# Sliding-window attention and a feed-forward: batch t+1 of the attention issued between the products of feed-forward tile t

## The chip, the core and the metric

The kernel runs on one core of a Trainium2 chip. Its time is the device time of one execution in microseconds (us). The engines of the core are TensorE (PE: matrix products, their weight loads shown apart as PEld), VectorE (DVE), ScalarE (ACT), GpSimd (POOL) and SyncE (SP, which only issues transfers here). [...]

## What is computed

q, k and v are [8, 8, 576, 64] in float32 (batch, head, position, head dimension). Each position attends to the 32 before and the 32 behind it, the result goes through a feed-forward of 512 to 2048 to 512 with the tanh form of gelu:

```
scores = q @ k.transpose(0, 1, 3, 2) / sqrt(64)
scores = where(abs(i - j) <= 32, scores, -1e9)
attn   = softmax(scores, axis=-1)
x = (attn @ v).transpose(0, 2, 1, 3).reshape(4608, 512)
h = x @ w_in                                             # [4608, 2048]
g = 0.5 * h * (1 + tanh(sqrt(2 / pi) * (h + 0.044715 * h * h * h)))
out = g @ w_out                                          # [4608, 512], float32
```

## The kernel before

It has two stages, one after the other. The attention loops over 32 pairs of heads (`for hp in range(NP)`). For a pair, SP loads q and k and GpSimd loads v (lines 143 to 147, v turned into fp16 on the way) in chunks of 128 positions. VectorE casts q and k to fp16 (L170, L171), TensorE transposes them (L175) and VectorE copies them back from PSUM (L177). For each head, TensorE multiplies each of five 128-key chunks with the 192 queries around it (L191: 64 rows of the array, as the head dimension is 64), ACT takes the exponential (L198), GpSimd multiplies with the band mask `bm` (L199), and TensorE multiplies the result with `vst`, which holds 64 columns of v and 64 columns of ones (L204): so 64 output partitions hold the sum over v, and 64 the sum of the weights. VectorE copies the latter (L206), ACT forms its reciprocal as exp(-ln) (L209, L211), and VectorE writes the product to `xT` (L214), the transposed input of the feed-forward, [128, 4, 4608] in fp16.

The feed-forward loops over 9 tiles of 512 tokens (L223). For each of 16 blocks of 128 hidden units, four products with `w_in16` (L228) make `ph`; ACT squares it (L232), VectorE forms the argument of a sigmoid (L234), ACT takes the sigmoid (L236), VectorE multiplies with `ph` (L237) into `gT`. For each of four blocks of 128 tokens, 16 products with `w_out16` (L241) make `py`; VectorE copies it (L244) and SP stores it (L245).

PSUM is split by stage: the attention's pools are closed before the feed-forward's is opened. The order of instructions on each engine is made by a scheduler that may move them: it sets products of L241 of one block between those of L228 of the next. The exponential and the logarithm share a table set that is loaded at the start (L65); the feed-forward's functions need another one.

Of the kernel before, what the change touches and what calls it, by code (L numbers as in the profile page):

```python
# [9 lines left out]
FP32 = mybir.dt.float32  # L10
FP16 = mybir.dt.float16
BF16 = mybir.dt.bfloat16
AF = mybir.ActivationFunctionType
ALU = mybir.AluOpType

_A = 0.044715
_K1 = 1.5957691216057308
_K3 = _K1 * _A
_C = 1.0 / _A

WINDOW = 32


@with_exitstack
def kernel(
# [9 lines left out]
    nc = tc.nc  # L35
    B, H, S, D = q.shape
    DM, DF = moe_w_in.shape
    NTOK = B * S
    NP = B * H // 2
    SCALE = 1.0 / float(D) ** 0.5  # L40
    assert S == 576 and D == 64 and DM == 512 and DF == 2048

    KC = 128
    NKC = 5
    QW = KC + 2 * WINDOW
    nky = [128, 128, 128, 128, 64]
    qws = [0, 96, 224, 352, 480]
    qwn = [192, 192, 192, 192, 96]
    scol = [0, 192, 384, 576, 768]

    qf = q.rearrange("b h s d -> (b h s d)")
    kf = k.rearrange("b h s d -> (b h s d)")
    vf = v.rearrange("b h s d -> (b h s d)")
# [3 lines left out]
    sb = ctx.enter_context(tc.tile_pool(name="sb", bufs=3))  # L57
    sbq = ctx.enter_context(tc.tile_pool(name="sbq", bufs=3))
    att_ctx = ExitStack()
    psA = att_ctx.enter_context(tc.tile_pool(name="psA", bufs=2, space=bass.MemoryType.PSUM))  # L60
    psO = att_ctx.enter_context(tc.tile_pool(name="psO", bufs=2, space=bass.MemoryType.PSUM))

    _tabs = list(get_activation_tables(nc.m.arch).keys())
    _set_id = _tabs.index("natural_log_exp_and_others")
    nc.scalar.add_instruction(mybir.InstLoadActFuncSet(  # L65
        name=nc.get_next_instruction_name(), act_func_set_id=_set_id, ins=[], outs=[]))

    idn = const.tile([128, 128], FP32, name="idn")
# [3 lines left out]
    idn16 = const.tile([128, 128], FP16, name="idn16")  # L72
    nc.vector.tensor_copy(idn16, idn)
    bm = const.tile([128, NKC, QW], FP16, name="bm")
    nc.gpsimd.memset(bm, 1.0)
    nc.gpsimd.affine_select(out=bm[:, 0, :], in_=bm[:, 0, :], compare_op=ALU.is_ge,
                            fill=0.0, base=32, pattern=[[1, QW]], channel_multiplier=-1)
    nc.gpsimd.affine_select(out=bm[:, 0, :], in_=bm[:, 0, :], compare_op=ALU.is_ge,
                            fill=0.0, base=32, pattern=[[-1, QW]], channel_multiplier=1)
    for kc in range(1, NKC):  # L80
        nc.gpsimd.affine_select(out=bm[:, kc, :], in_=bm[:, kc, :], compare_op=ALU.is_ge,
                                fill=0.0, base=0, pattern=[[1, QW]], channel_multiplier=-1)
        nc.gpsimd.affine_select(out=bm[:, kc, :], in_=bm[:, kc, :], compare_op=ALU.is_ge,
                                fill=0.0, base=64, pattern=[[-1, QW]], channel_multiplier=1)
    nc.gpsimd.affine_select(out=bm[:, 4, :], in_=bm[:, 4, :], compare_op=ALU.is_ge,
                            fill=0.0, base=63, pattern=[[0, QW]], channel_multiplier=-1)
    nc.gpsimd.affine_select(out=bm[:, 4, :], in_=bm[:, 4, :], compare_op=ALU.is_ge,
                            fill=0.0, base=95, pattern=[[-1, QW]], channel_multiplier=0)

    w_in16 = big.tile([128, 4, DF], FP16, name="w_in16")  # L90
    w_out16 = big.tile([128, 16, DM], FP16, name="w_out16")
    nc.gpsimd.dma_start(w_in16, moe_w_in.rearrange("(c p) f -> p c f", p=128))
    nc.gpsimd.dma_start(w_out16, moe_w_out.rearrange("(c p) f -> p c f", p=128))

    xT = big.tile([128, 4, NTOK], FP16, name="xT")

    raw = []
    for kc in range(NKC):
        lo = max(0, kc * KC - WINDOW)
        hi = min(S, kc * KC + nky[kc] + WINDOW)  # L100
        if lo < 512 < hi:
            raw.append((kc, lo, 512))
            raw.append((kc, 512, hi))
        else:
            raw.append((kc, lo, hi))
    segsA, segsB = [], []
    fA = fB = None
    for (kc, lo, hi) in raw:
        if lo < 512:
            if fA is None:  # L110
                segsA.append((kc, lo, hi, True)); fA = hi
            else:
                if lo < fA:
                    segsA.append((kc, lo, min(hi, fA), False))
                if hi > fA:
                    segsA.append((kc, max(lo, fA), hi, False)); fA = hi
        else:
            if fB is None:
                segsB.append((kc, lo, hi, True)); fB = hi
            else:  # L120
                if lo < fB:
                    segsB.append((kc, lo, min(hi, fB), False))
                if hi > fB:
                    segsB.append((kc, max(lo, fB), hi, False)); fB = hi
    od_segs = [(kc, a, b_, st, False) for (kc, a, b_, st) in segsA[:-1]] \
        + [segsA[-1][:3] + (segsA[-1][3], True)] \
        + [(kc, a, b_, st, False) for (kc, a, b_, st) in segsB[:-1]] \
        + [segsB[-1][:3] + (segsB[-1][3], True)]

    for hp in range(NP):  # L130
        b = hp // 4
        pb = hp % 4
        hA = 2 * pb

        qst = sb.tile([128, NKC, 2, 64], FP32, name="qst")
        kst = sb.tile([128, NKC, 2, 64], FP32, name="kst")
        vst = sbq.tile([128, NKC, 2, 128], FP16, name="vst")
        nc.gpsimd.memset(vst[:, :, :, 64:128], 1.0)
        for h2 in range(2):
            hh = (b * H + hA + h2)  # L140
            base = hh * S * D
            if hh < B * H - 1:
                nc.sync.dma_start(qst[:, :, h2, :],  # L143
                                  qf[base:base + 640 * 64].rearrange("(c p d) -> p c d", p=128, d=64))
                nc.sync.dma_start(kst[:, :, h2, :],  # L145
                                  kf[base:base + 640 * 64].rearrange("(c p d) -> p c d", p=128, d=64))
                nc.gpsimd.dma_start(vst[:, :, h2, 0:64],  # L147
                                    vf[base:base + 640 * 64].rearrange("(c p d) -> p c d", p=128, d=64))
            else:
                nc.sync.dma_start(qst[:, 0:4, h2, :],  # L150
                                  qf[base:base + 512 * 64].rearrange("(c p d) -> p c d", p=128, d=64))
                nc.sync.dma_start(qst[0:64, 4, h2, :],
                                  qf[base + 512 * 64:base + 576 * 64].rearrange("(p d) -> p d", d=64))
                nc.sync.dma_start(kst[:, 0:4, h2, :],
                                  kf[base:base + 512 * 64].rearrange("(c p d) -> p c d", p=128, d=64))
                nc.sync.dma_start(kst[0:64, 4, h2, :],
                                  kf[base + 512 * 64:base + 576 * 64].rearrange("(p d) -> p d", d=64))
                nc.gpsimd.dma_start(vst[:, 0:4, h2, 0:64],
                                    vf[base:base + 512 * 64].rearrange("(c p d) -> p c d", p=128, d=64))
                nc.gpsimd.dma_start(vst[0:64, 4, h2, 0:64],  # L160
                                    vf[base + 512 * 64:base + 576 * 64].rearrange("(p d) -> p d", d=64))
                nc.vector.memset(vst[64:128, 4, h2, 0:64], 0.0)
                nc.vector.memset(qst[64:128, 4, h2, :], 0.0)
                nc.vector.memset(kst[64:128, 4, h2, :], 0.0)

        QT = sbq.tile([128, 704], FP16, name="QT")
        KT = sbq.tile([128, 704], FP16, name="KT")
        qst16 = sbq.tile([128, NKC, 2, 64], FP16, name="qst16")
        kst16 = sbq.tile([128, NKC, 2, 64], FP16, name="kst16")
        nc.vector.tensor_copy(qst16, qst)  # L170
        nc.vector.tensor_copy(kst16, kst)  # L171
        for (stg, dst) in ((qst16, QT), (kst16, KT)):
            ptr = psA.tile([128, 1024], FP16, name="ptr", tag="SP")
# [102 lines left out]
```

## Time and profile before

| | before |
|---|---|
| median of 3 runs | 559.22 us (557.71 to 559.3) |
| profiled execution, span | 556.9 us |
| PE busy | 414.3 us (74%), 2560 products |
| DVE busy | 413.5 us (74%) |
| ACT busy | 261.9 us (47%) |
| POOL busy | 211.0 us (38%) |
| bytes moved | 40.29 MB, mean 72 GB/s |

The span runs from the first to the last instruction of the profiled execution. A busy PE is counted to the modelled end of each product, so products that overlap are counted once. "L228" is line 228 of the kernel. Text behind "<-" in a row's brackets names the engine and the line whose work ended the idle time ahead of the row.

### The profile page before, as it was taken

To read this page: it belongs to the slowest core of one execution; us is meant where nothing else is said; L and a number is where in the kernel's file an instruction comes from. 1 tells how busy PE (TensorE), PEld (TensorE's weight loads), DVE (VectorE), ACT (ScalarE), POOL (GpSimd) and SP (SyncE) were. 2 spreads that over 40 slices of the span, in tenths; PEclk is the share of its full clock that TensorE was granted. 3 is DMA by queue.
4 is the path that set the end of the run, shared out by engine and by line. 5 is a ranking of instruction groups with operands and counts; after the bars stand their busy time and mean duration, and the time that the engine had idled before them with its cause. 6 is when DMAs were issued, how large, how long until landed. Compare 5 with 4: busy or idle time off the path is not lost.

```text
span 556.9 us, 7306 instructions
## 1 busy us (share of the span) xinstructions
PE 414.3 (74%) x2560; PEld 228.6 (41%) x2560; DVE 413.5 (74%) x648; ACT 261.9 (47%) x418; POOL 211.0 (38%) x182
## 2 busy tenths in 40 slices
PE   0134666666666776665569999999999999999996
PEld 0123455444444554444334444344444443434342
DVE  2027877788888888888658686878878787868685
ACT  0112443334344434344347474747566574747472
POOL 7415988788998888888700000000000000000000
PEclk9999999999999999999999999999999999999999
DMA  8999467677668776753100201010010202020202
GB/s 179 200 191 209 65 84 95 95 113 102 102 101 118 118 105 102 114 69 24 14 0 1 75 1 57 21 57 20 17 58 2 75 2 75 2 75 1 75 2 76
DMA packets 133621, 40.29 MB, mean 72 GB/s; under 512 B 126416, under 2 KB 128464, under 8 KB 133584
## 3 DMA queue, kind: packets, MB, share of 16 engines
q1 hardware_dynamic: 89056, 30.39, 22.4%
q0 software_dynamic: 44528, 9.43, 19.0%
q8 instruction: 20, 0.33, 0.2%
q14 instruction: 17, 0.14, 0.1%
HBM read 39.80 MB, written 9.44 MB: 88 GB/s over the span
## 4 chain that ended last, share of the span: by engine, by line
PE 63%; DVE 21%; SPq 5%; issue 4%; DMA 3%; ACT 3%; DVEq 0%; ACTq 0%
PE py L241 22%; PE ph L228 21%; PE ps_od L204 12%; DVE kst L171 9%; PE ps_s L191 5%; DVE Dbuf L206 4%; PE ptr L175 3%; SPq L143 3%; DMA qst<-in_q_dram 2%; SPq L145 2%; DVE xT L214 2%; DVE gT L237 1%; DVE qst L170 1%; DVE uu L234 1%; ACT sq L232 1%
## 5 line engine op out<-in xcount | busy, mean ns | idle before, releaser
L199 POOL TENSOR_TENSOR PT<-PTr,bm 128x960 f16<-128x960 f16 x64 | 129.7, 2042 | 66.5 <-PE ps_od L204 43.4
L228 PE MATMUL ph<-xT,w_in 128*128 128x512 f16 x576 | 143.5, 383 | 14.1 <-DVE gT L237 10.2
L241 PE MATMUL py<-w_out,gT 128*128 128x512 f16 x576 | 141.0, 379 | 0.4 <-DVE yo L244 0.3
L232 ACT ACTIVATE sq<-ph 128x512 f16<-128x512 f32 x144 | 84.9, 589 | 79.0 <-PE ph L228 78.9
L234 DVE SCALAR_TENSOR_TENSOR uu<-sq,ph 128x512 f16<-128x512 f16 x144 | 98.3, 684 | 24.9 <-ACT sq L232 24.9
L198 ACT ACTIVATE PTr<-ps_s 128x960 f16<-128x960 f32 x64 | 58.8, 967 | 102.8 <-PE ps_s L191 88.8
L237 DVE SCALAR_TENSOR_TENSOR gT<-sg,ph 128x512 f16<-128x512 f16 x144 | 98.4, 684 | 11.4 <-ACT sg L236 6.8
L236 ACT ACTIVATE sg<-uu 128x512 f16<-128x512 f16 x144 | 90.3, 627 | 26.2 <-DVE uu L234 26.2
L228 PEld LDWEIGHTS <-w_in 128*128 128x128 f16 x576 | 56.5, 98 | 87.9 <-issue 26.6
L204 PE MATMUL ps_od<-PT,vst 128*128 128x64 f16 (+5 forms) x704 | 75.9, 251 | 13.7 <-DVE xT L214 13.7
L241 PEld LDWEIGHTS <-gT 128*128 128x128 f16 x576 | 54.8, 98 | 71.8 <-DVE gT L237 8.9
L204 PEld LDWEIGHTS <-vst 128*128 128x128 f16 (+1 forms) x704 | 59.8, 125 | 36.4 <-issue 23.4
L191 PE MATMUL ps_s<-QT,KT 64*128 64x192 f16 (+2 forms) x384 | 41.5, 330 | 43.8 <-DVE KT L178 38.8
L206 DVE COPY Dbuf<-ps_od 64x576 f32<-64x576 f32 x64 | 48.6, 760 | 28.9 <-PE ps_od L204 28.8
L175 PE MATMUL ptr<-idn,kst 128*128 128x128 f16 x160 | 23.0, 309 | 56.2 <-DVE kst L171 48.3
L171 DVE CAST kst<-kst 128x640 f16<-128x640 f32 x32 | 54.9, 1715 | 12.3 <-DMA kst<-in_k_dram 11.6
L209 ACT ACTIVATE Lt<-Dbuf 128x576 f32<-128x576 f32 x32 | 21.9, 683 | 75.7 <-DVE Dbuf L206 74.2
L147 POOL DMA_DIRECT2D vst<-in_v_dram x63 | 55.9, 889 | 0.0
L214 DVE TENSOR_TENSOR xT<-ps_od,Rt 64x576 f16<-64x576 f32 x64 | 47.1, 736 | 5.2 <-ACT Rt L211 4.2
L191 PEld LDWEIGHTS <-KT 64*128 64x128 f16 x384 | 28.5, 130 | 52.9 <-DVE KT L178 45.9
L244 DVE COPY yo<-py 128x512 f32<-128x512 f32 x36 | 23.2, 686 | 26.9 <-PE py L241 26.9
L170 DVE CAST qst<-qst 128x640 f16<-128x640 f32 x32 | 26.6, 831 | 20.5 <-DMA qst<-in_q_dram 19.6
(32 smaller groups left out, 146.6 us busy)
## 6 DMA issues: line engine op xcount, KB each, us to landing
qst<-in_q_dram SPq DMA_DIRECT2D x63, 160.0 KB, 3.5
kst<-in_k_dram SPq DMA_DIRECT2D x63, 160.0 KB, 3.1
out_dram<-yo SPq DMA_DIRECT2D x36, 256.0 KB, 2.1
vst<-in_v_dram POOLq DMA_DIRECT2D x63, 80.0 KB, 3.8
w_in<-in_moe_w_in_dram POOLq DMA_DIRECT2D x1, 2048.0 KB, 15.4
w_out<-in_moe_w_out_dram POOLq DMA_DIRECT2D x1, 2048.0 KB, 27.4
qst<-in_q_dram SPq DMA_DIRECT2D x1, 128.0 KB, 3.5
kst<-in_k_dram SPq DMA_DIRECT2D x1, 128.0 KB, 3.2
```

The costliest lines, as they stand in the source:

```text
L171: nc.vector.tensor_copy(kst16, kst)
L191: nc.tensor.matmul(ps_f[:, c0 + a:c0 + b_], KT[r0:r0 + 64, kc * KC:kc * KC + KC], QT[r0:r0 + 64, qws[kc] + a:qws[kc] + b_], start=True, st ...
L198: nc.scalar.activation(PTr, ps_s5, AF.Exp, scale=SCALE)
L199: nc.gpsimd.tensor_tensor(PT, PTr, bm, op=ALU.mult)
L204: nc.tensor.matmul(ps_od[:, a:b_], vst[0:nky[kc], kc, pi, :], mv, start=st, stop=lastf)
L206: nc.vector.tensor_copy(Dbuf[r0:r0 + 64, :], ps_od[64:128, 0:S])
L228: nc.tensor.matmul(ph, w_in16[:, dc, fc * 128:fc * 128 + 128], xT[:, dc, tt * 512:(tt + 1) * 512], start=(dc == 0), stop=(dc == 3))
L232: nc.scalar.activation(sq, ph, AF.Square)
L234: nc.vector.scalar_tensor_tensor(uu, sq, _C, ph, ALU.add, ALU.mult)
L236: nc.scalar.activation(sg, uu, AF.Sigmoid, scale=_K3)
L237: nc.vector.scalar_tensor_tensor(gT[:, fc, :], sg, 1.0, ph, ALU.mult, ALU.mult)
L241: nc.tensor.matmul(py, gT[:, fc, tc4 * 128:tc4 * 128 + 128], w_out16[:, fc, :], start=(fc == 0), stop=(fc == 15))
```

## The change

The two stages become one program in a fixed order (the scheduler no longer moves instructions). The attention of batch 0 comes first. Then feed-forward tile t is written with the attention of batch t+1 inside it, for t from 0 to 6; tiles 7 and 8 have none. In the tile's first half, the 16 blocks of products with `w_in`, stand casts and transposes; in its second half, 16 steps of four products with `w_out`, stand `scores` and `values` of eight units (a pair of heads and one half of the queries each).

The queries are stored in a strided order (column j*144 + p holds position 4p + j), so that a load of q or k has runs of 1 KB, and the output rows are stored back by the same rule. A unit multiplies three key chunks with 40, 48 and 16 columns of four strides, for two heads on 64 rows of the array each. Values are multiplied with 64 columns of v or of ones for two heads, each with its own 64 columns of the array and its own half of PSUM's partitions. The mask product moves from GpSimd to VectorE; the reciprocal of the sums is read from PSUM by ACT without a copy. Gelu becomes one ACT instruction, so the table set changes twice in each tile with attention; one load is written out at the start of its second half.

PSUM is shared: three banks for `ph` and `py`, two for the scores (one buffer), two for the values (one buffer), one for transposes.

```
-    for hp in range(NP):                 # the attention loop of before, lines 130 to 215
-        ...
-            nc.scalar.activation(sq, ph, AF.Square)
-            nc.vector.scalar_tensor_tensor(uu, sq, _C, ph, ALU.add, ALU.mult)
-            nc.scalar.activation(sg, uu, AF.Sigmoid, scale=_K3)
-            nc.vector.scalar_tensor_tensor(gT[:, fc, :], sg, 1.0, ph, ALU.mult, ALU.mult)
...
+PIECES = {
+    0: [(0, 0, 40), (1, 24, 72), (2, 56, 72)],
+    1: [(2, 72, 104), (3, 88, 136), (4, 120, 144)],
+}
...
+    psM = ctx.enter_context(tc.tile_pool(name="psM", bufs=3, space=PSUM))
+    psS = ctx.enter_context(tc.tile_pool(name="psS", bufs=1, space=PSUM))
+    psO = ctx.enter_context(tc.tile_pool(name="psO", bufs=1, space=PSUM))
+    psT = ctx.enter_context(tc.tile_pool(name="psT", bufs=1, space=PSUM))
+    ctx.enter_context(tc.manual_schedule(engines=None))
...
+    load_qk(0, 4)
+    ...
+    load_v(0)
+    for i in range(4):
+        nc.gpsimd.dma_start(w_in16[:, :, 512 * i:512 * i + 512], w_in_v[:, :, 512 * i:512 * i + 512])
+    for h in range(2):
+        ...                               # two masks, memset on VectorE, 13 selects on GpSimd
+    for i in range(4):
+        nc.gpsimd.dma_start(w_out16[:, 4 * i:4 * i + 4, :], w_out_v[:, 4 * i:4 * i + 4, :])
+    ...
+    load_qk(1, 1)
+    load_v(1)
...
+    def cast_pair(b, pr):
+        qr, kr, tr = raws[b]
+        ...
+        for src, dst in ((qr, q16), (kr, k16)):
+            nc.vector.tensor_copy(
+                dst.rearrange("p j h d -> p h j d"),
+                src[:, 2 * pr:2 * pr + 2, :].rearrange("p h (j d) -> p h j d", j=4))
+
+    def trans_pair(b, pr):
+        q16, k16 = halfs.pop((b, pr))
+        pt = psT.tile([128, 8, 128], FP16, name="pt", tag="T")
+        for j in range(4):
+            nc.tensor.transpose(pt[:, j, :], q16[:, j, :, :], idn)
+        for j in range(4):
+            nc.tensor.transpose(pt[:, 4 + j, :], k16[:, j, :, :], idn)
+        nc.vector.tensor_copy(QTs[b][:, pr, :, 0:128], pt[:, 0:4, :])
+        nc.vector.tensor_copy(
+            KTs[b % 2][:, pr, 0:512].rearrange("d (p j) -> d p j", j=4),
+            pt[:, 4:8, :].rearrange("d j p -> d p j"))
+
+    def scores(b, u):
+        pr, hf = u // 2, u % 2
+        ps = psS.tile([128, 2, 512], FP32, name="ps_s")
+        off = 0
+        for (c, p0, p1) in PIECES[hf]:
+            n = p1 - p0
+            for h in range(2):
+                r0 = 64 * h
+                nc.tensor.matmul(
+                    ps[:, h, off:off + 4 * n].rearrange("k (j p) -> k j p", j=4),
+                    KTs[b % 2][r0:r0 + 64, pr, 128 * c:128 * c + 128],
+                    QTs[b][r0:r0 + 64, pr, :, p0:p1],
+                    start=True, stop=True)
+            off += 4 * n
+        pe = ap_.tile([128, 2, SW], FP16, name="pe")
+        nc.scalar.activation(pe, ps[:, :, 0:SW], AF.Exp, scale=SCALE)
+        pm = ap_.tile([128, 2, SW], FP16, name="pm")
+        nc.vector.tensor_tensor(
+            pm, pe, masks[hf].rearrange("p (o w) -> p o w", o=1).broadcast_to([128, 2, SW]),
+            op=ALU.mult)
+        units[(b, u)] = pm
+
+    def values(b, u):
+        ...
+        od = psO.tile([128, 2, 512], FP32, name="ps_od")
+        ...
+        for i, (c, p0, p1) in enumerate(PIECES[hf]):
+            ...
+            for w in range(2):
+                for h in range(2):
+                    r0 = 64 * h
+                    nc.tensor.matmul(
+                        od[r0:r0 + 64, w, 0:4 * HALF].rearrange("d (j p) -> d j p", j=4)[:, :, a:e],
+                        V[:, c, 2 * pr + h, :] if w == 0 else ones,
+                        pm[:, h, off:off + 4 * n].rearrange("k (j p) -> k j p", j=4),
+                        start=(i == 0), stop=(i == last), skip_group_check=True)
+            off += 4 * n
+        lt = ap_.tile([128, 4 * HALF], FP32, name="lt")
+        nc.scalar.activation(lt, od[:, 1, 0:4 * HALF], AF.Ln)
+        rt = ap_.tile([128, 4 * HALF], FP32, name="rt")
+        nc.scalar.activation(rt, lt, AF.Exp, scale=-1.0)
+        nc.vector.tensor_tensor(
+            xT[:, pr, b * S:(b + 1) * S].rearrange("d (j p) -> d j p", j=4)[:, :, HALF * hf:HALF * hf + HALF],
+            ...
+
+    def ffn_in(t, fc):
+        ...
+        ph = psM.tile([128, 512], FP32, name="ph", tag="mm")
+        for dc in range(4):
+            nc.tensor.matmul(ph, w_in16[:, dc, fc * 128:fc * 128 + 128],
+                             xT[:, dc, t * 512:(t + 1) * 512],
+                             start=(dc == 0), stop=(dc == 3))
+        nc.scalar.activation(gTs[t][:, fc, :], ph, AF.Gelu_apprx_tanh)
...
+    cast_tail(0)
+    for pr in range(NPAIR):
+        cast_pair(0, pr)
+        trans_pair(0, pr)
+        if pr == 0:
+            trans_tail(0)
+        for u in (2 * pr, 2 * pr + 1):
+            scores(0, u)
+            if u > 0:
+                values(0, u - 1)
+    values(0, 7)
+
+    for t in range(NT):
+        b = t + 1
+        att = b < B
+        if att and b + 1 < B:
+            load_qk(b + 1, 1)
+            load_v(b + 1) if b + 1 >= 2 else None
+        for fc in range(NF):
+            if att:
+                if fc == 1:
+                    cast_tail(b)
+                    cast_pair(b, 0)
+                if fc == 2:
+                    trans_tail(b)
+                if fc in (4, 7, 10, 13):
+                    pr = (fc - 4) // 3
+                    trans_pair(b, pr)
+                    if pr < 3:
+                        cast_pair(b, pr + 1)
+            ffn_in(t, fc)
+        sched = {}
+        if att:
+            load_exp_table()
+            for u in range(8):
+                sched.setdefault((3 * u) // 2, []).append((scores, u))
+                sched.setdefault((3 * u) // 2 + 2, []).append((values, u))
+        for i in range(16):
+            for fn, u in sched.get(i, []):
+                fn(b, u)
+            ffn_out(t, i // 4, 4 * (i % 4), 4 * (i % 4) + 4)
```

`cast_tail` and `trans_tail` do the same for the last 64 positions of all heads: one cast, four transposes and five copies. `load_qk` issues transfers of q and k on SP, `load_v` five of v on GpSimd. `ffn_out` makes four products of one 128-token block per call, and copies and stores the block at its fourth call.

## Rows read from the trace of the kernel before

**Rows 1.** Busy us (instructions) by stage, then granted clock, DMA share, GB/s.

```profile
46.00:285.68 239.68, 146.32 (x1316) 109.00 (x1315) 197.45 (x298) 97.69 (x123) 189.18 (x149) 1.00 0.65 90
285.68:553.80 268.12, 256.77 (x1152) 111.19 (x1152) 205.06 (x324) 158.28 (x289) 0.00 (x0) 1.00 0.09 35
```

**Rows 2.** Timeline of a pair of heads: start us, us, engine, line, tiles, count.

```profile
158.20 1.28 PE L191 MATMUL ps_s<-QT,KT 64*128 64x192 f16 x12 [0.59 <-DVE KT L178]
159.41 2.26 PEld L204 LDWEIGHTS <-vst 128*128 128x128 f16 x22 [0.30 <-issue]
159.41 2.36 PE L204 MATMUL ps_od<-PT,vst 128*128 128x160 f16 x22
161.02 3.96 POOL L199 TENSOR_TENSOR PT<-PTr,bm 128x960 f16<-128x960 f16 x2
161.70 0.71 PE L175 MATMUL ptr<-idn,qst 128*128 128x128 f16 x5
...
167.25 1.28 PE L191 MATMUL ps_s<-QT,KT 64*128 64x192 f16 x12 [0.59 <-DVE KT L178]
```

**Rows 3.** Chain of waits, the same piece of two tiles: start us, us, what.

```profile
410.50 1.73 PE ph L228 x8
...
439.94 1.73 PE ph L228 x8
```

**Rows 4.** Timeline at a tile's boundary and at the end of the kernel.

```profile
438.48 1.02 PE L228 MATMUL ph<-xT,w_in 128*128 128x512 f16 x4 [1.20 <-DVE gT L237]
...
549.46 3.61 PE L241 MATMUL py<-w_out,gT 128*128 128x512 f16 x16 [0.35 <-DVE yo L244]
...
553.11 0.69 DVE L244 COPY yo<-py 128x512 f32<-128x512 f32 x1 [2.51 <-PE py L241]
```

**Rows 5.** Groups by line: tiles, shapes, count, busy us, mean ns, idle before.

```profile
L234 DVE SCALAR_TENSOR_TENSOR uu<-sq,ph 128x512 f16<-128x512 f16 x144 | 98.3, 684 | 24.9 <-ACT sq L232 24.9
L236 ACT ACTIVATE sg<-uu 128x512 f16<-128x512 f16 x144 | 90.3, 627 | 26.2 <-DVE uu L234 26.2
L232 ACT ACTIVATE sq<-ph 128x512 f16<-128x512 f32 x144 | 84.9, 589 | 79.0 <-PE ph L228 78.9
L198 ACT ACTIVATE PTr<-ps_s 128x960 f16<-128x960 f32 x64 | 58.8, 967 | 102.8 <-PE ps_s L191 88.8 <-POOL vst L138 14.0
L147 POOL DMA_DIRECT2D vst<-in_v_dram x63 | 55.9, 889 | 0.0
L171 DVE CAST kst<-kst 128x640 f16<-128x640 f32 x32 | 54.9, 1715 | 12.3 <-DMA kst<-in_k_dram 11.6
L214 DVE TENSOR_TENSOR xT<-ps_od,Rt 64x576 f16<-64x576 f32 x64 | 47.1, 736 | 5.2 <-ACT Rt L211 4.2
L170 DVE CAST qst<-qst 128x640 f16<-128x640 f32 x32 | 26.6, 831 | 20.5 <-DMA qst<-in_q_dram 19.6
L177 DVE COPY QT<-ptr 128x640 f16<-128x640 f16 x32 | 15.7, 491 | 3.7 <-PE ptr L175 2.8
```

**Rows 6.** Timeline where the feed-forward begins.

```profile
285.68 4.93 PE L228 MATMUL ph<-xT,w_in 128*128 128x512 f16 x12 [3.92 <-DVE xT L214]
286.06 0.15 PEld L228 LDWEIGHTS <-w_in 128*128 128x128 f16 x1 [0.27 <-issue]
286.49 0.15 PEld L228 LDWEIGHTS <-w_in 128*128 128x128 f16 x1 [0.28 <-issue]
...
288.19 1.28 ACT L236 ACT_TABLE_LOAD   x1
...
289.49 0.63 ACT L236 ACTIVATE sg<-uu 128x512 f16<-128x512 f16 x1
```

**Rows 7.** Timeline of the start: the first cast.

```profile
5.29 0.77 DVE L170 CAST qst<-qst 128x640 f16<-128x640 f32 x1 [4.28 <-DMA qst<-in_q_dram]
```

**Rows 8.** Busy us by stretch of the start, columns as in rows 1.

```profile
0.00:12.00 12.00, 1.23 (x10) 1.06 (x10) 3.85 (x8) 1.28 (x1) 9.92 (x24) 1.00 0.87 176
12.00:51.00 39.00, 10.00 (x83) 7.33 (x84) 12.12 (x21) 4.63 (x5) 16.12 (x13) 1.00 1.22 203
```

More of the change, by code (lines that the diff above doesn't have):

```diff
@@ L59 @@
[L59 to L68, printed above, removed]
+    rawp = ctx.enter_context(tc.tile_pool(name="rawp", bufs=2))
@@ new lines @@
+    ctx.enter_context(tc.manual_schedule(engines=None))
+    load_exp_table()
+    idn = const.tile([128, 128], FP16, name="idn")
+    ones = const.tile([128, 64], FP16, name="ones")
+    masks = [const.tile([128, SW], FP16, name=f"mask{h}") for h in range(2)]
+    KTs = [const.tile([128, NPAIR, 640], FP16, name=f"KT{i}") for i in range(2)]
+    Vs = [const.tile([128, 5, H, 64], FP16, name=f"V{i}") for i in range(2)]
+    w_in16 = big.tile([128, 4, DF], FP16, name="w_in16")
+    w_out16 = big.tile([128, NF, DM], FP16, name="w_out16")
@@ new lines, with load_qk @@
+    xT = big.tile([128, NPAIR, NTOK], FP16, name="xT")
+    raws = {}
+    def load_qk(b, split):
+        qr = rawp.tile([128, H, 256], FP32, name="qr")
+        kr = rawp.tile([128, H, 256], FP32, name="kr")
+        tr = rawp.tile([128, H, 64], FP32, name="tr")
+        raws[b] = (qr, kr, tr)
+        step = H // split
+        for h0 in range(0, H, step):
+            for src, dst in ((q, qr), (k, kr)):
+                nc.sync.dma_start(
+                    dst[:, h0:h0 + step, :],
+                    src[b, h0:h0 + step, 0:512, :].rearrange("h (p j) d -> p h (j d)", j=4))
+            if h0 == 0:
+                nc.sync.dma_start(tr[0:64, :, :], q[b, :, 512:576, :].rearrange("h s d -> s h d"))
+                nc.sync.dma_start(tr[64:128, :, :], k[b, :, 512:576, :].rearrange("h s d -> s h d"))
@@ L69, with load_v @@
+    def load_v(b):
+        V = Vs[b % 2]
+        for c in range(4):
+            nc.gpsimd.dma_start(V[:, c, :, :],
+                                v[b, :, 128 * c:128 * c + 128, :].rearrange("h p d -> p h d"))
+        nc.gpsimd.dma_start(V[0:64, 4, :, :], v[b, :, 512:576, :].rearrange("h p d -> p h d"))
+    w_in_v = moe_w_in.rearrange("(c p) f -> p c f", p=128)
+    w_out_v = moe_w_out.rearrange("(c p) f -> p c f", p=128)
+    load_qk(0, 4)
     nc.gpsimd.memset(idn, 0.0)
@@ L80 @@
[L80 to L124, printed above, removed]
@@ new lines @@
+    load_v(0)
+    for i in range(4):
+        nc.gpsimd.dma_start(w_in16[:, :, 512 * i:512 * i + 512], w_in_v[:, :, 512 * i:512 * i + 512])
+    for h in range(2):
+        m = masks[h]
+        nc.vector.memset(m, 1.0)
+        off = 0
+        for (c, p0, p1) in PIECES[h]:
+            n = p1 - p0
+            pp0 = p0 - (32 * c - 8)
+            mv = m[:, off:off + 4 * n].rearrange("k (j p) -> k j p", j=4)
+            nc.gpsimd.affine_select(out=mv, in_=mv, compare_op=ALU.is_ge, fill=0.0,
+                                    base=4 * pp0, pattern=[[1, 4], [4, n]], channel_multiplier=-1)
+            nc.gpsimd.affine_select(out=mv, in_=mv, compare_op=ALU.is_ge, fill=0.0,
+                                    base=64 - 4 * pp0, pattern=[[-1, 4], [-4, n]],
+                                    channel_multiplier=1)
+            if c == 4:
+                nc.gpsimd.affine_select(out=mv, in_=mv, compare_op=ALU.is_ge, fill=0.0,
+                                        base=63, pattern=[[0, 4], [0, n]], channel_multiplier=-1)
+            off += 4 * n
+        assert off == SW
@@ new lines, with cast_tail @@
+    for i in range(4):
+        nc.gpsimd.dma_start(w_out16[:, 4 * i:4 * i + 4, :], w_out_v[:, 4 * i:4 * i + 4, :])
+    nc.vector.memset(ones, 1.0)
+    for i in range(2):
+        nc.vector.memset(KTs[i][:, :, 576:640], 0.0)
+        nc.vector.memset(Vs[i][64:128, 4, :, :], 0.0)
+    load_qk(1, 1)
+    load_v(1)
+    halfs = {}
+    QTs = {}
+    def cast_tail(b):
+        t16 = hp.tile([128, H, 64], FP16, name="t16")
+        nc.vector.tensor_copy(t16, raws[b][2])
+        halfs[b] = t16
+        QTs[b] = ap_.tile([128, NPAIR, 4, NP_], FP16, name="QT")
@@ new lines, in trans_tail @@
+    def trans_tail(b):
+        t16 = halfs[b]
+        pt = psT.tile([128, NPAIR, 128], FP16, name="pt", tag="T", padded_shape=[128, 8, 128])
+        for pr in range(NPAIR):
+            nc.tensor.transpose(pt[:, pr, :], t16[:, 2 * pr:2 * pr + 2, :], idn)
+        for pr in range(NPAIR):
+            nc.vector.tensor_copy(
+                QTs[b][:, pr, :, 128:144],
+                pt[:, pr, 0:64].rearrange("d (p j) -> d j p", j=4))
+        nc.vector.tensor_copy(KTs[b % 2][:, :, 512:576], pt[:, :, 64:128])
@@ new lines @@
+    units = {}
+    def scores(b, u):
+        pr, hf = u // 2, u % 2
+        ps = psS.tile([128, 2, 512], FP32, name="ps_s")
+        off = 0
+        for (c, p0, p1) in PIECES[hf]:
+            n = p1 - p0
+            for h in range(2):
[13 more added lines that the diff above has]
+        units[(b, u)] = pm
@@ new lines, with ffn_out @@
+    pys = {}
+    def ffn_out(t, t4, f0, f1):
+        if f0 == 0:
+            pys[t4] = psM.tile([128, 512], FP32, name="py", tag="mm")
+        py = pys[t4]
+        for fc in range(f0, f1):
+            nc.tensor.matmul(py, gTs[t][:, fc, t4 * 128:t4 * 128 + 128], w_out16[:, fc, :],
+                             start=(fc == 0), stop=(fc == NF - 1))
+        if f1 == NF:
+            yo = yp.tile([128, 512], FP32, name="yo")
+            nc.vector.tensor_copy(yo, py)
+            g = t * 512 + t4 * 128
+            end = g + 128
+            m = 0
+            while g < end:
+                seg = g // NP_
+                e = min(end, (seg + 1) * NP_)
+                p0 = g - seg * NP_
+                nc.sync.dma_start(out_v[seg // 4, seg % 4, p0:p0 + e - g, :], yo[m:m + e - g, :])
+                m += e - g
+                g = e
```

171 lines of the change are left out of this document (37 added, 134 removed).

## Prediction

> **What bounds the kernel now.** I read the busy time of the stages first, then a pair of heads in order of time, then a tile of the feed-forward. In [rows 1], from 46 to 285.68 us, the attention runs alone: VectorE is busy 197 and GpSimd 189 of 240 us, TensorE 146 with short products. From 285.68 to 553.80 the feed-forward runs alone: TensorE 257 of 268 us, GpSimd 0. Each half idles what the other needs. [rows 2] show the attention: scores of two pairs start at 158.20 and 167.25; in between stand scores, GpSimd's mask products (3.96 us for two heads), value products and transposes, handed on from engine to engine. The feed-forward: the same piece of two tiles starts at 410.50 and 439.94 [rows 3], 29.4 us per tile. 16 products of 512 columns last 3.61 us [rows 4], so (3.61 - 0.38)/15 = 0.215 us each; four of them (a step, F below) are 0.86 us and a tile's 128 are 27.6 us. Most of the rest is one wait of 1.20 us for VectorE's gelu [rows 4].
>
> **The change, part by part.** The program becomes one fixed order: attention of batch 0 in the open, then 9 tiles, 7 of them with one batch's attention inside, 2 without. GpSimd keeps DMA issues and the masks.
>
> *Gelu.* Per 128x512 block two ACT passes (589 and 627 ns) and two VectorE passes (684 ns the first) [rows 5] become one ACT pass. That function isn't in the trace; its nearest row is the square, which also reads the block from PSUM and writes fp16 to SBUF: 589 ns, against 0.86 us of TensorE per block, so it hides with 0.27 us to spare. If it took 0.95 us, each of 144 blocks would lose 0.09 us, 13 in all. I put dry tiles at 27.6 us: 55.2 for two.
>
> *Table sets.* An exponential and a gelu set now alternate, 14 switches in 7 tiles. [rows 6] show one: 1.28 us, and the work behind it begins 1.30 us after the load. The load back to gelu stands behind the last unit's work, three steps (2.6 us) ahead of its user, and costs nothing; the other is on the path (below). [...]
>
> *TensorE's attention work.* A woven tile has 36 transposes and 8 units, each of 6 score products (832 columns, two heads in row tiles) and 12 value products (1664 columns, two heads in column tiles). In [rows 2] five transposes take 0.71 us, with the last one's 0.31 taken off 0.10 from one to the next; 12 scores of 1920 columns take 1.28 us and 22 value products of 1664 columns 2.36. By count that is 0.64 us of scores and 1.29 of values per unit. But the stage ran at the lower rate: behind it, the first 12 feed-forward products take 4.93 us and their weight loads stand 0.43 us apart [rows 6], twice the 0.215 reached later, though the granted clock reads 1.00 throughout [rows 1]. Amid dense products I halve: 0.32 and 0.65. No row has a column tile, or a row tile amid full ones. The nearest for changing shape is the 0.30 us in which weight loading idles between scores and values [rows 2]; some of it is the end of the last product, so I add 0.18 to the scores and 0.25 to the values: S = 0.5, V = 0.9. Ends: 0.32 and 0.35 (two heads truly side by side, changes free), 0.94 and 1.59 (lower rate plus all of 0.30). [...] At four turns of 0.30 a unit would be 2.2 us, not 1.4: 43 us more in 7 tiles. Transposes: between 0.05 and 0.107 us, I take 0.0625 near the lower end, 36 of them 2.25 us.
>
> *First half of a woven tile* (products with w_in, with casts and transposes): 16F + 2.25 = 16.0 us. VectorE's nine casts (831 ns or less each by L170 [rows 5], two thirds of that for 512 elements when undisturbed) and twelve copies (0.2 to 0.7) are some 13 us. A transpose stands three steps behind its cast, so I count no wait; what queues behind one is every feed-forward product. At L171's mean of 1.7 us per cast [rows 5] VectorE would need 22 us, 6 more than the half has, 42 us in all. That mean goes with GpSimd's products, which leave.
>
> *Second half* (products with w_out, 8 units): 16F + 8 x 1.4 = 25.0 us, plus waits, since one score buffer and one output buffer serve all units, and behind a waiting score or value product stands the next step. By the line through 512 and 960 columns [rows 5] an ACT pass of 832 takes 0.86 us; logarithm and exponential of 288 take 0.41 + 0.44; VectorE's product of 288 (736 ns for 576) 0.44; a handover 0.1, TensorE's end 0.2. The mask product moves to VectorE, between 0.63 us (at the rate of 640 fp16 in 491 ns) and 1.06 (576 in 736 ns); I take 0.7, and all of it hides under the steps between a unit's scores and its values. Then:
> - unit 1's scores wait for unit 0's exponential, behind the last gelu and the table load: 0.3 + 0.59 + 1.28 + 0.86 + 0.1 = 3.13, less S + F = 1.36: 1.77 us;
> - values of units 1, 3, 5, 7 wait for the output buffer: 0.3 + 0.85 + 0.1 + 0.44 + 0.1 = 1.79, less F: 0.92 us, four times;
> - scores of units 3, 5, 7 wait behind two ACT passes of the values ahead: 0.3 + 0.85 + 0.86 + 0.1 = 2.11, less 1.36: 0.75 us, three times.
> 7.7 us in all. Second half 32.7, woven tile 48.7, seven of them 341 us.
>
> *The start.* The first cast stood at 5.29 us [rows 7]; now 768 KB must land first, 4.4 us at the 176 GB/s of the first 12 us [rows 8], so 6.2. Casts, 12 transposes and tail copies: first scores at 12. GpSimd issues V and w_in first (9 at 0.89 us [rows 5]), so the masks come about 10.5 and 13, in time. A pair of heads then goes in series at the lower rate: casts 0.9, transposes 0.9, copies 1.1, S 0.65, twice (V 1.3, two ACT passes 0.85, product 0.44), handovers 1.4: 10.1 us; with the halved rates 8.8. Four pairs take 40 us, so the feed-forward starts near 51 (bounds 45 and 52). The queues: on GpSimd's, V, w_in, w_out and V of batch 1 follow each other, on SP's q and k of batches 0 and 1. Counted as they land, 7.4 MB stand up to the end of w_in and 10.1 MB up to V of batch 1; at 200 GB/s [rows 8] they are down at 37 and 51 us, needed at 51 and 70. Five us late would cost 5 us once. Later loads have a whole tile; a tile's loads stand ahead of its stores in SP's queue and wait for nothing in that tile.
>
> *The end.* From 553.11 [rows 4] to 556.9, copy and store, 3.8 us, as before.
>
> Sum: 51 + 341 + 55.2 + 3.8 = 451 us of span. The median of the runs is 559.2 for a span of 556.9, so 2.3 is added: **453 us**.
>
> **Rivals.**
> *A, the sum*: 453, its own range 425 to 485. Chance 0.70.
> *B, short products keep their measured cost*: 0.107, 0.65 and 1.3, with slightly longer waits, give 55.1 us per tile: 453 + 7 x 6.4 = 498; with 0.30 per turn on top, 529. For it: no row has them fast. Against: those rows are from the slow stage. Chance 0.14.
> *C, heads overlap fully*: 0.053, S 0.32, V 0.35; waits eat part of it: 5.4 us per tile less and 5 at the start: 410. For it: 1920 score columns in 1.28 us are quicker than one after the other at the lower rate. Chance 0.08.
> *D, slower than before: TensorE stays at its lower level in woven tiles.* F = 1.71, a tile 32F + 3.9 + 8 x 1.95 + 1 = 75 us, seven 526, in all 638. It decides once 106/7 = 15.1 of the 26.3 us per tile come, above 57% of woven time at the lower rate. For: the attention, TensorE busy 146 of 240 us, ended at that rate. Against: products of 512 columns fill 27.6 of 48.7 us, and waits of 1.20 us left the rate alone [rows 4]. Chance 0.05. [...]
> *E, the order doesn't overlap* (a wait sets the attention in series with the tiles): 12 + 8 x 40 + 248 + 6 = 586. Against: each unit's neighbours are steps that wait for nothing of it. Chance 0.03.
>
> **How the numbers follow.** The likeliest gives 453. The range 410 to 510 takes in C's time and B's, and leaves out D, E and the tails of B and C, about 0.15. This kernel's runs can tell 0.3% from no change. A, B and C are faster: 0.92. D near its point of decision is the same: 0.01. Slower: 0.07.
>
> **What would show it.** Right: 0.215 us between 512-column products inside woven tiles, a tile period near 49 us, some 8 us per tile of TensorE waiting for ACT and VectorE, dry tiles of 27.6, the first w_in product near 51 us. Wrong: 0.43 us between products (D), units of 2 us or more (B), gelu above 0.86 us, casts of 1.7 us, or TensorE waiting for a DMA in tile 0.

## The result and the profile after

The changed kernel takes 404.24 us (median of 4 runs, 402.94 to 404.56) beside 559.14 us for the one before: a ratio of 0.7235, interval 0.7215 to 0.7254. The forecast was 453 us with a range of 410 to 510. The direction was right; the time is below the range. The runs below bear out the mechanism of rival C.

The stages of the profile after, with columns as in [rows 1]: the attention of batch 0 in the open (with no feed-forward around it), the two halves of the second tile, which is woven (a batch's attention stands in it), and the first dry tile (without attention).

```profile
0.00:41.21 41.21, 15.94 (x181) 12.26 (x181) 18.73 (x44) 13.73 (x23) 19.36 (x37) 1.00 1.20 223
86.27:102.19 15.92, 15.92 (x101) 8.19 (x100) 8.61 (x23) 8.96 (x15) 0.00 (x0) 1.00 0.84 182
102.19:129.03 26.84, 21.83 (x210) 10.91 (x210) 10.20 (x19) 16.55 (x27) 4.20 (x5) 1.00 0.28 41
342.81:370.43 27.62, 27.62 (x129) 12.50 (x128) 2.77 (x4) 9.55 (x16) 0.00 (x0) 1.00 0.13 39
```

TensorE fills the first half and the dry tile completely, and 21.8 of the second half's 26.8 us. A woven tile is 15.92 + 26.84 = 42.76 us instead of 48.7. The next rows are the second half in order of time (start us, us, as in [rows 2]): the products with `w_out`, of which four make a step F, stand at line 260, scores at 197, values at 224.

```profile
102.19 0.35 PE L197 MATMUL ps_s<-QT,KT 64*128 64x160 f16 x6
102.48 1.04 PE L260 MATMUL py<-w_out,gT 128*128 128x512 f16 x4
105.12 0.36 PE L197 MATMUL ps_s<-QT,KT 64*128 64x128 f16 x6 [1.60 <-ACT pe L204]
105.41 1.04 PE L260 MATMUL py<-w_out,gT 128*128 128x512 f16 x4
106.38 0.26 PE L224 MATMUL ps_od<-pm,V 128*64 128x160 f16 x2
...
106.86 1.04 PE L260 MATMUL py<-w_out,gT 128*128 128x512 f16 x4
108.40 0.25 PE L224 MATMUL ps_od<-pm,V 128*64 128x128 f16 x2 [0.50 <-DVE xT L234]
...
108.89 0.35 PE L197 MATMUL ps_s<-QT,KT 64*128 64x160 f16 x6
109.17 1.04 PE L260 MATMUL py<-w_out,gT 128*128 128x512 f16 x4
110.68 0.36 PE L197 MATMUL ps_s<-QT,KT 64*128 64x128 f16 x6 [0.47 <-ACT pe L204]
```

Six scores take 102.48 - 102.19 = 0.29 us until the next product starts, twelve values 106.86 - 106.38 = 0.48, where S = 0.5 and V = 0.9 were forecast. Ahead of them the array changes its shape, from all rows and columns to halves; such a change is called a turn below. Where nothing waits, four products ahead of values take 106.38 - 105.41 = 0.97 us instead of F = 0.86, so a turn ahead costs 0.10 us more, which the 0.29 and 0.48 don't hold. The brackets are the three waits of the prediction, at the units where it put them, counted from the modelled end of the product ahead. By the starts of products, with S 0.29, V 0.48 and F 0.86, they are 1.78, 0.67 and 0.64 us (forecast 1.77, 0.92, 0.75); each of these holds a turn of 0.10 us. The view of TensorE's waits sums the two kinds over the kernel (us, times, longest):

```profile
PE ps_s L197 <- ACT pe L204: 22.0, 29, 1.6
PE ps_od L224 <- DVE xT L234: 17.9, 32, 1.5
```

The ACT groups behind them and the one-pass gelu (columns as in [rows 5]), then one table load in order of time, answering [rows 6]:

```profile
L250 ACT ACTIVATE gT<-ph 128x512 f16<-128x512 f32 x144 | 86.0, 597 | 80.8 <-PE ph L247 80.8
L204 ACT ACTIVATE pe<-ps_s 128x832 f16<-128x832 f32 x64 | 54.8, 857 | 35.2 <-PE ps_s L197 35.1
L206 DVE TENSOR_TENSOR pm<-pe,mask 128x832 f16<-128x832 f16 x64 | 37.9, 592 | 59.6 <-ACT pe L204 58.2 <-POOL mask L131 0.6
```

```profile
102.30 0.60 ACT L250 ACTIVATE gT<-ph 128x512 f16<-128x512 f32 x1 [0.27 <-PE ph L247]
102.91 1.28 ACT L55 ACT_TABLE_LOAD   x1
104.20 0.86 ACT L204 ACTIVATE pe<-ps_s 128x832 f16<-128x832 f32 x1
```

Gelu takes 597 ns (forecast 589), the exponential 857 (860), the mask product 592 (700), a table switch 104.20 - 102.90 = 1.30 us from the gelu's end to the exponential's start (1.30). So single passes were forecast within 20 ns, but for the mask product; what failed lies in TensorE's short products.

### The profile page after: what moved, and what is told of

The parts are those of the page before. It is cut to its first block, busy times and chain, and to the rows that moved or that the text cites. A ratio compares the mean times of both kernels' runs of the same rounds, so it can differ in the third digit from the quotient of the medians.

```text
span 402.5 us, 6406 instructions
## 1 busy us (share of the span) xinstructions
PE 337.8 (84%) x2592; PEld 171.4 (43%) x2592; DVE 156.7 (39%) x347; ACT 213.5 (53%) x352; POOL 45.0 (11%) x67
## 2 busy tenths in 40 slices
DMA packets 72574, 37.64 MB, mean 94 GB/s; under 512 B 47456, under 2 KB 67936, under 8 KB 72544
## 4 chain that ended last, share of the span: by engine, by line
PE 67%; ACT 19%; DVE 6%; issue 4%; POOL 3%; ACTq 0%; POOLq 0%
PE ph L247 31%; PE py L260 20%; PE ps_od L224 9%; ACT pe L204 7%; ACT lt L231 6%; DVE xT L234 4%; ACT rt L233 4%; PE ps_s L197 3%; ACT L55 2%; PE pt L179 2%; PE pt L181 2%; POOL V L103 1%; POOL w_in L116 1%; POOL mask L125 1%; POOL mask L127 0%
## 5 line engine op out<-in xcount | busy, mean ns | idle before, releaser
L250 ACT ACTIVATE gT<-ph 128x512 f16<-128x512 f32 x144 | 86.0, 597 | 80.8 <-PE ph L247 80.8
L204 ACT ACTIVATE pe<-ps_s 128x832 f16<-128x832 f32 x64 | 54.8, 857 | 35.2 <-PE ps_s L197 35.1
L260 PEld LDWEIGHTS <-gT 128*128 128x128 f16 x576 | 48.8, 97 | 54.4
L206 DVE TENSOR_TENSOR pm<-pe,mask 128x832 f16<-128x832 f16 x64 | 37.9, 592 | 59.6 <-ACT pe L204 58.2
L234 DVE TENSOR_TENSOR xT<-ps_od,rt 128x288 f16<-128x288 f32 x64 | 29.3, 458 | 66.4 <-ACT rt L233 66.4
L231 ACT ACTIVATE lt<-ps_od 128x288 f32<-128x288 f32 x64 | 26.2, 410 | 52.3 <-PE ps_od L224 52.3
L103 POOL DMA_DIRECT2D V<-in_v_dram x32 | 28.6, 901 | 204.3 <-PE ps_od L224 178.5
L224 PE MATMUL ps_od<-pm,V 128*64 128x192 f16 (+4 forms) x384 | 35.7, 240 | 18.1 <-DVE xT L234 17.9
L224 PEld LDWEIGHTS <-V 128*64 128x64 f16 x384 | 26.1, 115 | 42.3 <-issue 42.2
L224 PE MATMUL ps_od<-pm,ones 128*64 128x192 f16 (+4 forms) x384 | 33.4, 236 | 0.0
L233 ACT ACTIVATE rt<-lt 128x288 f32<-128x288 f32 x64 | 28.3, 442 | 2.0
L183 DVE COPY KT<-pt 128x512 f16<-128x512 f16 x32 | 21.8, 681 | 0.0
```

The costliest lines, as they stand in the source:

```text
L103: nc.gpsimd.dma_start(V[:, c, :, :], v[b, :, 128 * c:128 * c + 128, :].rearrange("h p d -> p h d"))
L204: nc.scalar.activation(pe, ps[:, :, 0:SW], AF.Exp, scale=SCALE)
L206: nc.vector.tensor_tensor(pm, pe, masks[hf].rearrange("p (o w) -> p o w", o=1).broadcast_to([128, 2, SW]), op=ALU.mult)
L224: nc.tensor.matmul(od[r0:r0 + 64, w, 0:4 * HALF].rearrange("d (j p) -> d j p", j=4)[:, :, a:e], V[:, c, 2 * pr + h, :] if w == 0 else ones ...
L231: nc.scalar.activation(lt, od[:, 1, 0:4 * HALF], AF.Ln)
L233: nc.scalar.activation(rt, lt, AF.Exp, scale=-1.0)
```

## Experiments

Three of them change the new kernel's order or leave one thing out (e1, e2, e5); e4 does one part alone on the kernel before; e3 is a new spacing; and e6 to e10 stand on e3, because in its tiles after the first TensorE hardly waits (one gap of 0.07 us per tile), so that a cost shows undiluted.

### Are the values short because two heads run side by side? (e1, e2)

```
-        for i, (c, p0, p1) in enumerate(PIECES[hf]):
...
-            for w in range(2):
-                for h in range(2):
...
+        for h in range(2):                           # e1: head outermost
...
+            for i, (c, p0, p1) in enumerate(PIECES[hf]):
...
+                for w in range(2):
...
```

e2 sets `scores` by head in the same way.

> All twelve value products of a unit stay, in another order: all of one head first, then the other, so that neighbours use the same 64 columns of the array. If two heads run side by side in the array (theory H), a unit's values grow from 0.49 us by their other half at full rate, 832 columns or 0.35 us: 56 units in tiles 19.6 us, 8 in the open at the lower rate about 4, in all about 427 us (420 to 432). If the values are short only because the rate is high and a change of shape is nearly free (theory R), order doesn't matter: 404 us, within 1.

Measured: 412.88 us, 8.6 more than the changed kernel, not 23.

> The same for the six score products: three of one head, then three of the other, so that neighbours use the same 64 rows. Theory H: a unit's scores grow from 0.285 us by 416 columns, 0.17 us, less what the last and first product of two heads still share: 56 times, and about 1.5 us in the open: 412 us (408 to 416). Theory R: 404 us, within 1.

Measured: 403.53 us, the same as without the edit, not 412. Both miss theory H's number, and e2 gives R's. The trace of e1 shows why that doesn't decide it. One unit's values in order of time:

```profile
107.24 0.26 PE L225 MATMUL ps_od<-pm,V 128*64 128x160 f16 x1
107.33 0.23 PE L225 MATMUL ps_od<-pm,ones 128*64 128x160 f16 x1
107.40 0.26 PE L225 MATMUL ps_od<-pm,V 128*64 128x192 f16 x2
...
107.89 0.61 PE L261 MATMUL py<-w_out,gT 128*128 128x512 f16 x2
```

The first two products stand alone (x1 where the changed kernel has x2), but the third has a partner: the instruction starts are 107.399 for the first head's third product (192 columns) and 107.405 for the second head's first (160 columns), which is seventh in the order, ahead of the fourth at 107.48. TensorE started products of the other half of the array ahead of earlier ones, so the starts aren't in the program's order here. In e2 the two heads' products of 128 columns, first and fourth in the order, start 12 ns apart, ahead of the second and third:

```profile
104.20 0.24 PE L198 MATMUL ps_s<-QT,KT 64*128 64x128 f16 x2 [1.60 <-ACT pe L205]
```

So an order by heads didn't put them in series; e6 and e7 take the halves themselves away. In e1 the heads overlap in part: the unit's values take 107.89 - 107.24 = 0.65 us instead of 0.48, and 56 x 0.17 = 9.5 us is about what the run lost.

### Side by side, measured by taking the halves away (e6, e7)

The edit of e7 is `r0 = 0` in `scores`; that of e6, beside `ones` widened to 128 columns and the flags of a sum that both heads now share:

```
-                        od[r0:r0 + 64, w, 0:4 * HALF]...[:, :, a:e],
-                        V[:, c, 2 * pr + h, :] if w == 0 else ones,         # 64 columns
+                        od[:, w, 0:4 * HALF]...[:, :, a:e],
+                        V[:, c, 2 * pr:2 * pr + 2, :] if w == 0 else ones,  # 128 columns
```

> Based on the kernel with evenly set units (368.1 us), in which TensorE waits for nothing in a tile's second half. The twelve value products of a unit use all 128 columns of the array (v of both heads, or 128 columns of ones) and all 128 output partitions, so that two can't run side by side and the array isn't reshaped for them; the two heads' sums are thereby mixed, which is the part that it leaves out. Count and moving columns are the same. Theory H (side by side halves them; each reshaping costs 0.10 us): 1664 columns at full rate are 0.69 us instead of 0.36, less two turns of 0.10: 0.13 us more per unit, 56 units 7 us, and about 5 at the start at the lower rate: 380 us (376 to 385). Theory R (rate and weight loads set the time, no overlap): only the turns go, 368 - 56 x 0.2 = 357 us.

> Based on the evenly set kernel (368.1 us). All six score products of a unit use rows 0 to 63 of the array: the second head's scores are left out and the first's computed twice. Theory H: 832 columns in series at full rate, 0.35 instead of 0.17 us: 56 x 0.17 = 10 us, and 2 at the start: 380 us (376 to 384). Theory R: 368 us, within 1.

Measured: e6 381.48 us, e7 378.79 us; a tile is 38.90 us in e6 (first products with `w_in` at 87.04 and 125.94 us) and 39.06 in e7 (83.34 and 122.40), where e3's is 37.64 (81.21 and 118.85), so 0.16 and 0.18 us more per unit. Both are theory H's numbers; R would have had e6 at 357. Values in e6, then scores in e7, in order of time:

```profile
107.32 0.30 PE L223 MATMUL ps_od<-pm,V 128*128 128x160 f16 x2
...
108.04 0.81 PE L259 MATMUL py<-w_out,gT 128*128 128x512 f16 x3
```

```profile
102.63 0.53 PE L197 MATMUL ps_s<-QT,KT 64*128 64x128 f16 x6
103.10 1.04 PE L260 MATMUL py<-w_out,gT 128*128 128x512 f16 x4
```

On the whole array twelve values take 108.04 - 107.32 = 0.72 us, what 1664 columns need at 0.215 us per 512 (0.70). On column halves they took 0.48, with the turn back to the whole array in it. Six scores on one row half take 0.47 us, not 0.29. So the saving by two heads side by side is real here, 0.18 us for the six scores and 0.24 for the twelve values.

### What a turn costs (e8, e9)

e8 sets a unit's first four values one product with `w_out` ahead of the other eight; e9 sets the scores of units 2 to 7 directly behind values:

```
-            for u, at in enumerate((0, 13, 20, 26, 32, 38, 44, 50)):   # e3
+            for u, at in enumerate((0, 13, 17, 23, 29, 35, 41, 47)):   # e9
```

> Based on the evenly set kernel (368.1 us). A unit's first four value products stand one product with w_out ahead of its other eight, so that the array changes shape twice more per unit, with nothing else added. Theory S (a change of shape costs about 0.10 us of TensorE): 56 x 0.2 = 11 us more, 379 us (375 to 384). Theory F (changes are free, and the 0.10 us between the last value and the next product is only the end of a short product): 368 us, within 1.

> As the evenly set kernel (368.1 us), but the scores of units 2 to 7 stand directly behind the values of units 0 to 5 (before products 17, 23, 29, 35, 41 and 47), so that one change of shape per such pair is saved. Theory S (0.10 us per change): 7 tiles x 6 x 0.1 = 4 us less, 364 us (362 to 365), if the chains still hide. Theory F (changes free): 368 us. If the scores come too early for the single buffer, waits return and it is slower than 368 us.

Measured: e8 382.05 us, 13.9 more than e3; e9 363.45 us, 4.7 less. A tile of e8 is 39.7 us on average (82.05 to 320.38 us for six) against 37.64: 2.06/8 = 0.26 us per unit for two turns, 0.13 each; a tile of e9 37.00 (79.34 to 116.34), 0.64/6 = 0.11 for each turn saved. Theory S holds in both directions. In e8 one sees the single product between two turns:

```profile
102.53 0.23 PE L229 MATMUL ps_od<-pm,ones 128*64 128x160 f16 x2
102.70 0.39 PE L268 MATMUL py<-w_out,gT 128*128 128x512 f16 x1
103.02 0.27 PE L229 MATMUL ps_od<-pm,V 128*64 128x192 f16 x2
```

From its start to the next value product are 0.32 us; on its own it would be 0.215.

### Where TensorE's waits came from (e3)

```
-                sched.setdefault((3 * u) // 2, []).append((scores, u))
-                sched.setdefault((3 * u) // 2 + 2, []).append((values, u))
+                sched.setdefault(17 + 6 * u, []).append((values, u))
+            for u, at in enumerate((0, 13, 20, 26, 32, 38, 44, 50)):
+                sched.setdefault(at, []).append((scores, u))
-        for i in range(16):
+        for i in range(64):
...
```

> The eight units of a tile are set evenly among the 64 products with w_out: values of unit u before product 17 + 6u, scores before products 0, 13, 20, 26, 32, 38, 44 and 50; nothing else changes. If TensorE's waits in the second half (1.78 + 4 x 0.67 + 3 x 0.64 = 6.4 us per tile by the starts of products) come from uneven spacing in front of single buffers (theory W), they go almost wholly: 404 - 7 x 6.2 = 361 us (356 to 368), a tile period near 36.6 us. If the single buffers or ACT can't serve a unit faster whatever the order (theory B), the waits turn up at other units and the time stays above 390 us.

Measured: 368.12 us, 36 less than the changed kernel, 0.1 us above theory W's range and far from B's. The same two kinds of waits, over the whole execution:

```profile
PE ps_od L224 <- DVE xT L234: 3.9, 4, 1.5
...
PE ps_s L197 <- ACT pe L204: 1.0, 1, 1.0
```

4.9 us where the changed kernel had 39.9, and all of it in the start and in no tile. A tile came down by 5.1 us, not by the 6.4 of waits: eight turns of 0.10 us that stood in the waits stay, each even unit now makes four turns, while the old order set values and scores of neighbouring units together three times per tile (0.3 us), and one gap is left. An even unit in order of time:

```profile
102.07 0.82 PE L260 MATMUL py<-w_out,gT 128*128 128x512 f16 x3
102.82 0.35 PE L197 MATMUL ps_s<-QT,KT 64*128 64x160 f16 x6
103.11 0.82 PE L260 MATMUL py<-w_out,gT 128*128 128x512 f16 x3
103.86 0.25 PE L224 MATMUL ps_od<-pm,V 128*64 128x128 f16 x2
```

Three products take 0.75 us up to the scores or values behind them, 0.105 more than 3 x 0.215. With 0.29 and 0.48 a unit by itself costs TensorE 0.98 us, four turns included, not 1.4.

### Which part of the change brought how much (e4, e5)

e4 replaces lines 231 to 237 of the kernel before by `nc.scalar.activation(gT[:, fc, :], ph, AF.Gelu_apprx_tanh)`. e5 writes tile t without attention and sets batch t+1's behind it in batch 0's order.

> The kernel before with gelu as one ACT pass, nothing else changed. The prediction's reading of its dry tiles: a tile goes from 29.4 to 27.6 us, 9 x 1.8 = 16 us less, 543 us (539 to 547); then gelu explains a tenth of the whole gain. If VectorE's passes held up more than the waits show (theory V), the feed-forward falls below 27.6 us per tile or the time below 535 us, which the products' 0.215 us would forbid.

> The changed kernel with its attention of batch t+1 taken out of tile t and set behind it, in the order that batch 0 has. Everything else (row and column tiles, one-pass gelu, strided order) stays. Theory K (keeping TensorE fed while the chains run is the gain): a batch in the open costs 33 us as at the start (four pairs at 7.7 and the last values), so 41 + 7 x 33 + 9 x 27.7 + 4 = 525 us (515 to 540), 120 us above the woven kernel. Theory L (the attention itself has become cheap): much of the gain stays, below 480 us.

Measured: e4 543.00 us, as forecast to the microsecond; its chain of waits in the feed-forward has nothing but TensorE in it, 27.62 us per tile:

```profile
385.90 13.81 PE py L235 x64
399.71 13.81 PE ph L228 x64
413.52 13.81 PE py L235 x64
```

e5 534.22 us, in theory K's range. So of 155 us, gelu alone gives 16 (558.81 to 543.00 in one comparison), the smaller attention and its other casts, masks and tiles about 9 more (543 to 534), and weaving 130. That is against an open attention in batch 0's order, which isn't the best one: e10 below begins the first tile 4.8 us earlier by another order, so beside seven such batches weaving would be worth some 96 us, an estimate (130 - 7 x 4.8) that no run tests. A batch in the open takes 61.5 - 27.6 = 34 us with the slow start of the tile behind it; woven it adds 15. In e5 the granted clock differs between a stretch of the open attention and a stretch of the tile behind it:

```profile
75.00:105.00 30.00, 15.67 (x169) 11.39 (x167) 14.05 (x33) 14.41 (x25) 4.09 (x5) 0.52 0.38 87
...
105.50:133.00 27.50, 27.30 (x123) 12.02 (x121) 2.23 (x4) 10.52 (x17) 0.00 (x0) 0.97 0.28 40
```

It was 0.52 in the first, where TensorE was busy 15.7 of 30 us, and 0.97 in the second, where it was busy 27.3 of 27.5.

### The start (e10)

```
...
-        for u in (2 * pr, 2 * pr + 1):               # batch 0: casts, transposes, then two units
...
+    for u in range(8):
+        scores(0, u)
+        if u % 2 == 0 and u < 6:
+            trans_pair(0, u // 2 + 1)
+        if u > 0:
+            values(0, u - 1)
+        if u % 2 == 1 and u < 5:
+            cast_pair(0, u // 2 + 2)
```

> As the run with units back to back, and in the attention of batch 0 the casts and transposes of the next pair of heads are set ahead of the current pair's units. If the 7.7 us per pair at the start are one chain in series (my sum's reading), taking casts and transposes out of it leaves some 2.2 us per unit: 12.3 + 8 x 2.2 + 1.5 = 32 us instead of 41, so 9 us less than the run beside it, about 355 us (352 to 359). If w_in's arrival sets the start of tile 0, it stays within 2 us of the run beside it.

Measured: 357.84 us, 5.6 less than e9: inside the range of the first theory, but short of its 9 us. The first tile starts at 35.86 us instead of 40.66. The arrival of `w_in` isn't the limit, but a unit takes more than 2.2 us:

```profile
24.30 0.61 PE L179 MATMUL pt<-idn,q 128*128 128x128 f16 x4 [1.34 <-DVE q L170]
...
27.91 0.35 PE L224 MATMUL ps_od<-pm,V 128*64 128x160 f16 x2 [1.01 <-DVE xT L234]
...
30.29 0.31 PE L224 MATMUL ps_od<-pm,V 128*64 128x128 f16 x2 [1.01 <-DVE xT L234]
```

Two values with no transposes between them stand 2.38 us apart, held by the one output buffer; and where a pair's transposes stand, TensorE waits 1.34 us for casts that queue behind the product into `xT` on VectorE. This is the fastest kernel of the study, 0.640 of the kernel before (0.639 to 0.641) and 11% below the changed one.

## Why the prediction missed, step by step

*Bound of the kernel before, and the direction*: right. Each stage left idle what the other needed; beside e5's open order, weaving brings 130 of the 155 us.

*Gelu and the dry tiles*: right. 27.62 us against 27.6, e4 at 543.00 us.

*Table sets*: right. A switch cost 1.30 us in all, as in [rows 6], and the wait of unit 1 came out at 1.78 us by that price (forecast 1.77, with a longer S).

*First half of a woven tile*: right, 15.92 against 16.0 us. Casts took 0.44 us, less than two thirds of 831 ns, and no transpose in a tile waited for one. In the kernel before, the cast of L171 took 0.62 us at 5.97 and 0.49 at 18.96, ahead of GpSimd's first mask product at 22.1, but 3.29 us at 162.60, beside the mask products of [rows 2]; here GpSimd is busy 0.00 us in this half. Thirteen copies stand there, not the twelve that were counted.

*TensorE's attention work*: here it failed. The term S + V = 1.4 us was 0.29 + 0.48, and with 56 units that is 0.63 x 56 = 35 of the 48.5 us between the forecast span of 451 and the measured 402.5. (With the turns ahead, 0.10 us each, a unit by itself costs 0.98; in this kernel half of these turns stand in the waits.) The step that failed is the count by products that was then halved: it took time per product from a stage at the lower rate and halved it. That time held that stage's own turns, and for values weights for one head at a time, with no product beside it. Counting columns of the longer head would have given 416 x 0.42 ns = 0.17 and 832 x 0.42 = 0.35 us, and one turn of 0.12 behind each comes to 0.29 and 0.47; with one more ahead of each it is 1.0, where 0.98 was measured. I had 0.35 as the lower end for values and read the overlap of scores off the same rows, then gave the case a chance of 0.08. e6 and e7 show that the overlap is there; e8 and e9 that a turn costs 0.11 to 0.13 us, so the 0.18 and 0.25 that I added for two turns each were of the right size, and the 0.30 us idle of weight loading that I had set beside a turn was too much for one.

*The waits*: the mechanism was right at every unit, the sum 6.4 instead of 7.7 us per tile, 9 us in seven tiles. The handovers that I put at 0.1 us each, an estimate that no row shows, are 0.03 between ACT passes and VectorE (the output buffer's chain takes 108.40 - 106.86 = 1.54 us from the product behind the last value to the next value, not 1.79). e3 shows that they belong to the spacing.

*The start*: 41.2 instead of 51 us, 9.8 of the 48.5. First scores came at 12.31 us (forecast 12), but a pair of heads takes 7.2 to 8.0 us, not 10.1. The same two terms were in it: by the starts of products, values at the lower rate are 0.84 us (40.37 to 41.21), not 1.3, and scores 0.46 (19.48 to 19.94), not 0.65, together 1.1 us per pair; the rest isn't taken apart here. And tile 0 began while the last unit's ACT passes still ran, since its first products need other rows of `xT`; its first products at the lower rate and the wait for those rows cost it 45.06 - 42.76 = 2.3 us, which the sum didn't have.

*The end and the queues*: right. 402.5 - 398.2 = 4.3 us against 3.8, and no wait of TensorE for a transfer in any tile.

*Rivals*: C (410 us, for fully overlapping heads) was the case, and even its time was a little high, since it kept the forecast's waits and handovers. B's cost per product appears nowhere (its 529 counted two turns of a unit; with the four that the prediction counts elsewhere it is 565). D didn't happen: inside woven tiles 512-column products stand 0.215 us apart, four of them in 1.04 us with the last one's 0.38. E is the order that e5 runs: 534 us, where E's price was 586, again too dear by the price of the units.

The pieces put together: 7 x 5.9 for the second halves (35 from units and 9 from waits, less 3 for the turns ahead of units that don't wait), 9.8 for the start, less 2.3 for tile 0: 48.8, against 48.5 measured.

## What to carry to other kernels

Where short products use independent halves of the array, as here, cost them by the columns of the longer half and add something for each change of shape, there and back: 0.42 ns a column and 0.12 us a change (0.13 in e8, 0.11 in e9) come to 1.0 us for a unit of this kernel, where 0.98 was measured. Don't scale a time per product out of a stage with another rate and other shapes: that gave 1.4 us. When a phase with a long chain can be set between products that wait for nothing, its own cost may drop, here from 34 us per batch (e5) to 15, and the order within still counts: even spacing behind single buffers was worth another 36 us (e3), with no instruction changed.

## What the hardware showed beyond that

- TensorE started products out of the program's order where they use another half of the array: in e1 the seventh product starts 6 ns after the third, in e2 the fourth 12 ns after the first. Setting these products one head after the other didn't put them in series: a unit's values took 0.65 us in e1, where theory H's count for products in series gives 0.49 + 0.35 = 0.84.
- The granted clock in the profile doesn't show the lower rate of the start. It reads 1.00 there, where the first eight 512-column products of tile 0 take 3.83 us; eight in the next tile take 1.89. The trace's own records of the clock begin only at 45.68 us, where the starts of these products go from 0.43 to 0.22 us apart, and in the kernel before at 290.14 us, behind the whole attention: what reads 1.00 ahead of that has no record. In e5 the same attention in the open, later in the run, shows 0.52. For the start, the spacing of products is the only sign.

```profile
41.21 3.83 PE L247 MATMUL ph<-xT,w_in 128*128 128x512 f16 x8
...
86.27 1.89 PE L247 MATMUL ph<-xT,w_in 128*128 128x512 f16 x8
```
